# Another order for the first third of an attention and two-MLP kernel

## The chip, the cores and the metric

The kernel runs on one core of a Trainium2 chip. The metric is the device time of one execution in microseconds (us). A core has TensorE (matrix products and transposes, PE in the profile, with its weight loads as PEld), VectorE (DVE), ScalarE (ACT), GpSimd (POOL) and SyncE (SP), which here issues nearly all DMAs. Each engine takes its instructions in the order in which the program gives them and waits where an operand or a buffer isn't ready; the engines run beside each other.

## The reference, cut to what matters

```python
# q, k, v: (2, 8, 768, 64)
k_sum = max of k over blocks of 32;  v_sum = mean of v over blocks of 32
scores_l = q k^T / 8, kept where |i - j| < 16
scores_s = q k_sum^T / 8 + log(32)
a = softmax over [scores_l, scores_s], as exp / (sum + 1e-9)
x = (a @ [v, v_sum]) as (1536, 512)
h = x @ w_in;  x = (h * sigmoid(h)) @ w_out          # d_ff 2048
out = ((x @ w_a) * (x @ w_b)) @ w_out2               # d_ff 1536
```

The weights of the MLPs come in double precision.

## The kernel before, in words

**Attention** runs in 24 steps, 12 for each of the two batches; a step takes 64 queries of all 8 heads against a window of 96 keys and the 24 block maxima. Steps 0 to 7 feed the first block of 512 tokens, 8 to 15 the second, 16 to 23 the third.

**The first MLP** runs in 48 slots, 16 of w_in's columns blocks for each block of tokens: `m1` multiplies x with 128 columns of w_in, `sg` takes the SiLU, `m2` multiplies the gate with 128 rows of w_out. To keep accuracy, each operand is split into a high part (a rounded copy) and a low part (the rest), and a product is three matmuls for each 128 x 128 of weights. Weights come as words of a double: `da` (ScalarE) and `du` (VectorE) decode a tile from its staging buffer, `dj` (VectorE) joins the two, and w_out's tiles are stored to DRAM (`SP`) and loaded again (`RO`) for later blocks of tokens. Decoded tiles share three buffers (`w32`), staged words four (`stage`).

**The order** of all this, up to the last step of the attention and slot 27, is written out by hand as a list of words, `ORDER`, that is run from left to right (lines 28 to 79 and 898 to 923). A word is a name with its numbers, and for many the engine at its end (`a` ScalarE, `v` VectorE, `p` GpSimd). On an engine the instructions stand in the order of the words that put work on it. The names that matter here:

- `LQq`, `LKq`: a quick load of 256 queries or keys of a batch (512 KB, one DMA), reordered by `br`; `LQ`, `LK`: the same in two slower DMAs. `LG`: values for the block means; `LV:n`: the values of step n, into one of four buffers `vw`; `LI`, `LO`: words of a tile of w_in or w_out.
- `tq`, `tk`: transposes of queries and keys on TensorE; `bq` scales queries out of PSUM; `wk` copies keys into windows (ScalarE); `mk`, `sk`, `pk` make block maxima and put them beside the keys.
- `sv`, `mv`, `kv`: block means of v: adds, products, and a copy out of PSUM into the first `vw` buffer; `PV:i` sends it by DMA into buffer i.
- Step n: `sc` scores, `sm` mask and minimum or maximum (VectorE), `su` subtracts it (only for steps outside `ACTS`), `ex` exponentials (ScalarE), `rs` sum plus 1e-9 and reciprocal, `no` multiplies, `tr` transposes, `pc` copies out of PSUM, `av` multiplies with the values, `xh` and `xl` write the high and low part of x.
- `hi`, `lo`: high and low part of a decoded tile; `hR`, `lR`: the same for a tile loaded again; `gh`, `gl`: high and low part of a gate.

For a step in `ACTS`, `ex` is four exponentials, each with its sum and a subtraction folded in; for another it is one, and VectorE sums. In `rs` the 1e-9 stands in a column beside the sums, and one VectorE reduction adds the two:

```python
        nc.vector.tensor_reduce(st[:, 3, :], ap_of(st, NPR, [[1, NPR], [NPR, 2]]), op=ALU.add, axis=AX.X)
        nc.vector.reciprocal(st[:, 3, :], st[:, 3, :])
```

After `ORDER` a loop does slots 28 to 47 and then the second MLP, which forms its products from seven instead of eight block products; its order is not part of the change.

Of the kernel before, what the change touches and what calls it, by code (L numbers as in the profile page):

```python
# [36 lines left out]
av:3 LV:4 no:7:p ex:8 xh:3:v xl:2 tr:4 LV:5 LI:4 LV:7 LV:6 da:in:0 no:6:p pc:5:v sc:9 pc:4:a xl:3 da:in:4 dj:in:1 tr:6  # L37
LI:2 sm:9 sc:11 hi:in:1:a av:5 sm:11 av:4 pc:6:a tr:7 pc:7:a xh:5:a rs:8 LK:1:1 av:6 xh:4:v LO:0 LQ:1:0 lo:in:1:p ex:11
dj:in:0 av:7 hi:in:0:v m1:1:0 xl:5 xh:7:a xl:4 xh:6:v rs:11 du:in:4 xl:6 xl:7 no:8:v LV:8 sc:10 lo:in:0:p sm:10 m1:0:0
m1:1:1 ok:1 tr:8 ex:9 sg:1:p tq:1:0:0 pc:8:a dj:in:4 rs:9 m1:0:1 no:11:v av:8 da:in:2 hi:in:4:a du:in:2 su:10:p du:in:3  # L40
tk:1:1:0 no:9:v LI:6 tr:9 gh:1:p LK:1:2 LO:1 dj:in:2 bq:1:0:0:a tq:1:0:1 da:in:3 LI:8 lo:in:4:v dj:in:3 xh:8:a sg:0:v
# [5 lines left out]
lo:in:5:v gl:2:p m1:6 mk:1:0:0 LI:7 mk:1:2:0 tk:1:0:1 gl:3:v da:out:4 hi:out:3:a lo:out:3:p sg:6:v mk:1:0:1 SP:1 da:in:8
du:out:4 dj:in:8 wk:1:0:1 LO:6 m2:2 m2:3 sk:1:v SP:3 hi:in:8:a pk:1:0:v du:in:7 LO:5 LI:9 dj:out:4 lo:in:8:p wk:1:0:0
da:in:7 LV:11 da:out:6 sc:13 LO:8 dj:in:7 gh:6:v m1:5 du:out:6 gl:6:v du:out:5 dj:out:6 hi:in:7:a lo:in:7:v LI:10
hi:out:4:a m1:8 sm:13 su:13:p sg:5:v sc:14 SP:4 du:in:9 gh:5:a da:in:9 LO:7 gl:5:v LV:9 lo:out:4:v hi:out:6:a lo:out:6:p  # L50
dj:in:9 LV:10 m1:7 du:in:10 sm:14 sc:12 da:out:5 hi:in:9:v lo:in:9:p ex:10 rs:10 no:10:p LG:1:2 sg:8:v m2:4 sg:7:p sm:12
da:in:10 dj:out:5 dj:in:10 av:9 SP:6 hi:out:5:a lo:out:5:v LI:11 LI:13 xh:9:a du:out:8 ex:14 xl:9 da:out:7 gh:8:v m2:5
hi:in:10:v LQ:1:1 du:out:7 gh:7:a sv:1:2:1:p m2:6 rs:14 dj:out:7 SP:5 hi:out:7:a lo:in:10:v lo:out:7:v LG:1:3 da:out:8
ex:12 da:in:13 ex:13 sv:1:3:1:p gl:7:v tr:10 SP:7 dj:out:8 pc:10:a mv:1:2:256:1 du:in:13 LG:1:0 m1:9 sg:9:v gl:8:v
du:in:11 gh:9:a da:in:11 LO:9 sv:1:1:1:p dj:in:13 rs:13 m1:10 du:out:9 dj:in:11 hi:out:8:a av:10 mv:1:3:0:1 lo:out:8:v
LI:12 kv:1:2:a m2:7 xh:10:a LO:13 du:in:12 hi:in:11:a sg:10:v LI:15 hi:in:13:a lo:in:13:p xl:10 da:out:9 SP:8 lo:in:11:v
sc:15 sm:15 tq:1:1:0 pk:1:1:a bq:1:1:0:a dj:out:9 rs:12 hi:out:9:a gh:10:a av:11 du:in:15 gl:9:v m2:8 da:in:12 tq:1:1:1
xh:11:v LO:10 bq:1:1:1:a gl:10:v xl:11 su:15:v no:14:p m1:11 da:in:15 sv:1:0:1:v tr:14 dj:in:15 mv:1:0:256:1 mv:1:1:0:1
LV:12 LO:11 SP:9 kv:1:0:v sg:11:v pc:14:a no:12:p hi:in:15:v m1:13 sc:18 LO:12 gh:11:a pk:1:2:a du:out:10 ex:15 LV:13
dj:in:12 hi:in:12:a lo:out:9:p no:13:v m2:9 sm:18 gl:11:v du:out:11 da:out:10 LI:14 lo:in:12:p sg:13:p tr:12 gh:13:a  # L60
pc:12:a da:out:11 dj:out:11 du:out:13 dj:out:10 PV:1:2 hi:out:10:a lo:in:15:p m1:12 du:in:14 lo:out:10:p PV:1:3 sc:16
LV:14 sm:16 LV:15 da:in:14 rs:15 av:12 SP:10 xh:12:v tr:13 xl:12 hi:out:11:v no:15:v pc:13:a LO:15 LO:14 lo:out:11:v
da:out:13 LV:16 PV:1:1 SP:11 dj:in:14 hi:in:14:v da:out:12 m2:10 lo:in:14:v dj:out:13 av:14 xh:14:a sg:12:v gh:12:v
gl:12:v xl:14 hi:out:13:a tr:15 da:out:14 m1:15 du:out:12 m2:11 gl:13:p pc:15:a dj:out:12 SP:12 sg:15:v hi:out:12:v
av:13 LV:17 lo:out:13:p ex:16 av:15 xh:15:a xl:15 LQ:1:2 SP:13 lo:out:12:p m1:14 du:out:15 da:out:15 du:out:14 gh:15:v
dj:out:14 xh:13:a hi:out:14:v m2:12 sg:14:p xl:13 sc:17 sm:17 gl:15:v m1:17 dj:out:15 gh:14:v sc:19 lo:out:14:p sm:19
# [1069 lines left out]
```

## Time and profile before

| | |
|---|---|
| median of 3 runs | 628.45 us (626.63 to 632.15) |
| profiled execution | 628.75 us, of which span 627.0 us |
| TensorE busy in the span | 608.3 us (97%) |
| VectorE, ScalarE, GpSimd busy | 395.4 us (63%), 294.2 us (47%), 276.1 us (44%) |
| granted TensorE clock, mean | 0.993 of full speed |

The span runs from the first to the last instruction of the profiled execution. The shares are averages over stages with different limits; a busy TensorE may still be waiting inside a group of matmuls. Times below are us from the span's start.

### The profile page before, as it was taken

The numbers are of one execution on the slowest core, as the hardware profiler recorded it, in microseconds if no ns is written. First come the engines' busy times: TensorE is split into PE (matmuls) and PEld (weight loads), VectorE is DVE, ScalarE is ACT, GpSimd is POOL, SyncE is SP. The second block draws the span as 40 slices with busy tenths as digits, with TensorE's granted clock in tenths as the row PEclk, the third lists the DMA queues.
The fourth block names the chain that finished last, engine by engine and source line by source line (L and its number), as shares of the span: only waits on it lengthen the run. The fifth ranks groups of instructions, "written<-read, shape, count | busy, mean of one in ns | idle before, by whom it ended". The sixth has DMA issues, their size and how long they took to land.

```text
span 627.0 us, 10081 instructions
## 1 busy us (share of the span) xinstructions
PE 608.3 (97%) x3630; PEld 525.0 (84%) x3630; DVE 395.4 (63%) x767; ACT 294.2 (47%) x636; POOL 276.1 (44%) x263
## 2 busy tenths in 40 slices
...
GB/s 227 213 238 230 277 271 283 160 179 161 56 38 103 38 98 143 244 204 212 178 160 155 114 51 106 175 158 166 110 227 84 202 35 84 80 217 306 119 0 135
DMA packets 90522, 97.82 MB, mean 156 GB/s; under 512 B 39000, under 2 KB 68440, under 8 KB 90472
## 3 DMA queue, kind: packets, MB, share of 16 engines
...
q14 instruction: 21, 0.17, 0.1%
...
## 4 chain that ended last, share of the span: by engine, by line
PE 88%; DVE 4%; DMA 3%; ACT 3%; issue 1%; SPq 0%; POOL 0%; DVEq 0%; ACTq 0%
PE h L562 20%; PE y L595 19%; PE bankh L806 13%; PE bankg L806 13%; PE ol L853 10%; PE o L832 5%; PE av L466 2%; PE sc L387 1%; PE pt L452 1%; ACT sm L431 1%; DMA vw<-vw 1%; PE kt L259 1%; DMA st_in<-in_moe_w_in_dram 1%; PE qt L259 1%; DMA st_q<-in_q_dram 1%
## 5 line engine op out<-in xcount | busy, mean ns | idle before, releaser
L562 PE MATMUL h<-x,w_in 128*128 128x512 f32 (+1 forms) x600 | 141.7, 386 | 1.1 <-issue 0.9
L595 PE MATMUL y<-g,w_out 128*128 128x512 f32 x576 | 139.8, 394 | 0.8 <-issue 0.8
L595 PEld LDWEIGHTS y<-g,w_out 128*128 128x128 f32 x576 | 106.9, 188 | 25.0 <-issue 2.1
L562 PEld LDWEIGHTS h<-x,w_in 128*128 128x128 f32 x600 | 108.0, 188 | 23.4 <-issue 1.4
L539 POOL TENSOR_TENSOR w_out<-re_out,w_out 128x512 fp32r<-128x512 f32 x36 | 50.5, 1404 | 111.9 <-ACT w_out L148 101.0
L853 PE MATMUL ol<-w_out,plh 128*128 128x512 f32 x192 | 59.1, 389 | 0.0
L577 DVE TENSOR_TENSOR g<-h,g 128x512 fp32r<-128x512 f32 x31 | 21.4, 689 | 39.1 <-ACT g L148 38.9
L539 POOL TENSOR_TENSOR w_out<-w_out,w_out 128x512 fp32r<-128x512 f32 x20 | 27.9, 1407 | 37.0 <-ACT w_out L148 21.8
L570 ACT ACTIVATE h<-h 128x512 f32<-128x512 f32 x31 | 18.1, 584 | 54.7 <-PE h L562 54.7
L853 PEld LDWEIGHTS ol<-w_out,plh 128*128 128x128 f32 x192 | 36.0, 188 | 7.5
L771 POOL TENSOR_TENSOR ab<-sum,ab 128x384 f32<-128x384 f32 x24 | 27.9, 1170 | 30.9 <-DVE sum L768 30.7
L148 ACT CAST w_out<-re_out 128x512 fp32r<-128x512 f32 x37 | 23.0, 622 | 31.4 <-issue 26.0
L853 PE MATMUL ol<-w_out,pll 128*128 128x512 f32 x96 | 37.3, 389 | 0.0
L845 DVE TENSOR_TENSOR pll<-pl,plh 128x1024 fp32r<-128x1024 f32 x12 | 16.9, 1406 | 31.0 <-ACT plh L844 31.0
L832 PE MATMUL o<-w_out,p 128*128 128x512 f32 x108 | 29.9, 394 | 0.0
L516 DVE SCALAR_TENSOR_TENSOR w_out<-w_out,u_out 128x512 uint32<-128x512 uint32 x28 | 24.8, 885 | 7.8 <-ACT w_out L506 6.8
L806 PE MATMUL bankh<-yhT,wab 128*128 128x384 f32 x96 | 28.4, 336 | 0.0
L577 POOL TENSOR_TENSOR g<-sg,g 128x512 fp32r<-128x512 f32 x10 | 13.7, 1378 | 28.4 <-ACT g L148 15.6
L417 DVE CUSTOM_DVE_ANT_0 sm<-sc,mask 128x120 f32<-128x120 f32 x76 | 16.9, 277 | 12.6 <-PE sc L387 12.6
L749 ACT COPY sum<-bankh 128x384 f32<-128x384 f32 x12 | 5.8, 479 | 39.9 <-PE bankh L806 39.9
L683 POOL TENSOR_TENSOR wab<-c,wab 128x768 fp32r<-128x768 f32 x6 | 11.3, 1878 | 28.2 <-ACT wab L680 28.2
L506 ACT ACTIVATE w_out<-st_out 128x512 f32<-128x512 f32 x28 | 18.8, 670 | 6.5 <-DVE w_in L539 3.4
...
## 6 DMA issues: line engine op xcount, KB each, us to landing
...
```

What stands on the lines that cost most here:

```text
L148: nc.scalar.copy(o, i)
L506: nc.scalar.activation(w32, stage_t[kind, f][:, :, 1].bitcast(F32), AF.Prelu, scale=2.0 ** -112, alpha=2.0 ** 32)
L516: nc.vector.scalar_tensor_tensor(bits, bits, 3, u_t.pop((kind, f)), op0=ALU.logical_shift_left, op1=ALU.bitwise_or)
L539: engine.tensor_tensor(w[:, 1], w32_t[kind, f], w[:, 0].bitcast(F32), op=ALU.subtract)
L562: nc.tensor.matmul(h_ps[i][:, cols], win_t[f][:, a, c * P:(c + 1) * P], x_t[n][:, steps, m, c, :], start=(idx == 0), stop=(idx == 3 * NK - 1))
L570: nc.scalar.activation(sg_t[i], ps, AF.Silu)
L577: engines[engine].tensor_tensor(g_t[i][:, 1], sg_t.pop(i), g_t[i][:, 0].bitcast(F32), op=ALU.subtract)
L595: nc.tensor.matmul(y_ps[n, c], wout_t[i][:, a, c * P:(c + 1) * P], g_t[i][:, m, :], start=(f == 0 and (a, m) == (0, 0)), stop=(f == N1 - 1 ...
L771: engines["v" if k == 6 else "p"].tensor_tensor(at, x, at, op=ALU.mult)
L806: nc.tensor.matmul((A, B)[b], weights(u, a, s, s + 1)[:, 0, c * P:(c + 1) * P], yc_t[q, y][m][:, c, :], start=(idx == 0 and not more), sto ...
L832: nc.tensor.matmul(o_ps[t], g[:, a, c:c + P], w[:, m], start=(begins and (a, m) == (0, 0)), stop=(ends and (a, m) == PARTS[-1]))
L853: nc.tensor.matmul(late_o[j], late_p[f][a][:, j * P:(j + 1) * P], wo2_t[N2 + f][:, m], start=(f == 0 and (a, m) == (0, 0)), stop=(f == N2 ...
```

## The change: what it does

The words of `ORDER` are put in another order and some get another engine. Nothing after `ORDER` is changed. In particular:

- The first queries (`LQq:0:0`) are loaded by two DMAs of four heads each instead of one, and `br:q` copies them in two halves (both on ScalarE).
- At the start: `br:k:0:0` comes ahead of `bq:0:0:1` on VectorE, and `bq:0:0:1` moves to ScalarE; `br:k:0:1` moves from ScalarE to VectorE, `bq:0:1:1` from ScalarE to VectorE. On SyncE, `LG:0:0` comes ahead of `LV:0`, and `PV:0:2 PV:0:1 LV:2 LI:3 LV:3 PV:0:3` becomes `PV:0:1 PV:0:2 PV:0:3 LI:3 LV:2 LV:3`.
- Steps 16 and 19 leave `ACTS`: their exponential is one instruction, GpSimd subtracts (`su:16:p`, `su:19:p`), VectorE sums.
- In `rs:6`, `rs:12` and `rs:21` GpSimd adds the 1e-9 between two VectorE instructions.
- The number of words that put work on GpSimd goes from 61 to 77: among them `hi:out:1`, `hi:out:13`, `hR:23`, `hR:26` (high parts of tiles), `gh:17`, `gh:18` (of gates), the low parts `lR:16`, `lR:18`, `lR:20`, `lR:22`, `lR:26`, `lo:in:14`, `gl:26`, the products `no:13` and `no:15`, and the subtractions `su:16`, `su:17`, `su:19`, `su:21`. `hi:out:0` and `gh:1` leave it for ScalarE, `lo:out:2` and `lo:in:8` for VectorE.
- In the middle: `da:out:3`, `gh:2` and `hi:out:3` come ahead of `da:in:5` on ScalarE, and `LI:5` behind `SP:0`, `LK:1:0` and `LO:3` on SyncE. On TensorE the order differs in some places, among them `sc:20 m1:18 av:17` for `sc:20 av:17`, with `m2:14` ahead of `m1:18`.

```diff
-ACTS = {0, 1, 2, 3, 4, 5, 6, 7, 8, 9, 11, 12, 14, 16, 18, 19, 20, 23}
+ACTS = {0, 1, 2, 3, 4, 5, 6, 7, 8, 9, 11, 12, 14, 18, 20, 23}
...
 ORDER = """
-LQq:0:0 br:q:0:0:a LKq:0:0 ok:0 tq:0:0:1 LKq:0:1 LKq:0:2 LG:0:1 bq:0:0:1:v sv:0:1:1:p br:k:0:0:v tk:0:0:1 tk:0:0:0
-tq:0:0:0 br:k:0:1:a mk:0:0:0 tk:0:1:1 mk:0:1:1 wk:0:0:1 LQ:0:1 tk:0:1:0 qz wk:0:0:0 br:k:0:2:v LV:0 tk:0:2:1 mk:0:0:1
+LQq:0:0 br:q:0:0:a tq:0:0:1 ok:0 LKq:0:0 LKq:0:1 LKq:0:2 br:k:0:0:v LG:0:1 bq:0:0:1:a sv:0:1:1:p tk:0:0:1 tk:0:0:0
+wk:0:0:1 br:k:0:1:v tq:0:0:0 tk:0:1:1 mk:0:0:0 tk:0:1:0 mk:0:1:1 LQ:0:1 wk:0:0:0 qz br:k:0:2:v mk:0:0:1 tk:0:2:1
...
-sv:0:2:1:p mv:0:2:0:1 no:2:p kv:0:0:a rs:0 no:0:v pc:1:v PV:0:2 sc:3 tq:0:2:0 tr:0 sc:4 PV:0:1 sm:3 da:in:1 bq:0:2:0:a
-du:in:0 sm:4 ex:3 pc:0:v tq:0:2:1 tr:2 ex:4 sc:7 bq:0:2:1:v av:1 rs:3 no:3:p av:0 tr:3 LV:2 sm:7 rs:5 no:5:p pc:2:a
-xh:1:a rs:4 xh:0:a no:4:p xl:1 sc:6 pc:3:v ex:7 xl:0 sm:6 LI:3 ex:6 rs:7 LV:3 av:2 tr:5 sc:8 sm:8 PV:0:3 xh:2:a rs:6
+sv:0:2:1:p no:2:p pc:1:v mv:0:2:0:1 kv:0:0:a rs:0 sc:3 tq:0:2:0 no:0:v PV:0:1 tr:0 bq:0:2:0:a sc:4 sm:3 ex:3 pc:0:v sm:4
+du:in:0 tq:0:2:1 tr:2 sc:7 ex:4 da:in:1 av:1 rs:3 av:0 PV:0:2 pc:2:a rs:5 no:3:p bq:0:2:1:v tr:3 sm:7 no:5:p rs:4 PV:0:3
+sc:6 LI:3 no:4:p xh:0:a LV:2 LV:3 xh:1:a pc:3:v ex:7 xl:1 sm:6 ex:6 xl:0 rs:7 av:2 xh:2:a tr:5 sc:8 sm:8 rs:6:p av:3
...
-hi:in:6:a SP:0 du:in:5 lo:in:6:v wk:1:2:1 wk:1:2:0 da:out:2 dj:out:2 LK:1:0 LO:3 m2:0 sg:3:p lo:out:1:v hi:out:2:v
-gh:3:a du:in:8 SP:2 lo:out:2:p da:in:5 da:out:3 m2:1 LG:1:1 dj:in:5 hi:in:5:a du:out:3 dj:out:3 tk:1:0:0 gh:2:a
+lo:in:6:v da:out:2 sg:2:p LK:1:0 wk:1:2:0 dj:out:2 m2:0 wk:1:2:1 lo:out:1:v LO:3 hi:out:2:a LI:5 du:in:8 lo:out:2:v SP:2
+da:out:3 du:out:3 LG:1:1 dj:out:3 du:in:5 gh:2:a tk:1:0:0 m2:1 mk:1:0:0 LI:7 gl:2:p m1:6 hi:out:3:a mk:1:2:0 tk:1:0:1
...
-m2:15 yh:0:2 gh:16:p yh:0:0 lR:16:v ex:19 first no:18:p pc:17:v sc:20 sm:20 av:17 rs:19 RO:19 tr:18 gh:18:a LV:21
...
+no:17:v tr:17 gh:16:p first lR:16:p no:16:p pc:17:v no:18:p m2:15 yh:0:2 sc:20 yh:0:0 yh:0:1 sm:20 gl:17:v m1:18 sg:18:p
+yh:0:3 RO:19 av:17 rs:19 tr:18 gh:18:p xh:17:v gl:18:p gl:16:v pc:18:a m1:21 xl:17 no:19:p sc:22 sm:22 RO:23 sg:21:p
...
 """
...
-            nc.sync.dma_start(st, src.rearrange("h (p r) d -> p h (r d)", r=2))
+
+            n = 2 if (kind, b, t) == ("q", 0, 0) else 1
+            for i in range(n):
+                hs = slice(i * H // n, (i + 1) * H // n)
+                nc.sync.dma_start(st[:, hs], src[hs].rearrange("h (p r) d -> p h (r d)", r=2))
...
     def bring(kind, b, t, engine):
-        copy(engine, *quick_t.pop((kind, b, t)))
+        o, i = quick_t.pop((kind, b, t))
+        if kind == "q":
+            copy(engine, o[:, :, 0:H // 2], i[:, :, 0:H // 2])
+            copy(engine, o[:, :, H // 2:], i[:, :, H // 2:])
+        else:
+            copy(engine, o, i)
...
-    def rs(n):
+    def rs(n, engine="v"):
         sm, st, _ = sm_t[n]
         if not by_act(n):
             nc.vector.tensor_reduce(st[:, 1, :], sm, op=ALU.add, axis=AX.X)
-
-        nc.vector.tensor_reduce(st[:, 3, :], ap_of(st, NPR, [[1, NPR], [NPR, 2]]), op=ALU.add, axis=AX.X)
+        if engine == "p":
+            nc.gpsimd.tensor_scalar_add(st[:, 3, :], st[:, 1, :], 1e-9)
+        else:
+
+            nc.vector.tensor_reduce(st[:, 3, :], ap_of(st, NPR, [[1, NPR], [NPR, 2]]), op=ALU.add, axis=AX.X)
         nc.vector.reciprocal(st[:, 3, :], st[:, 3, :])
```

## Rows read from the trace of the kernel before

**Rows 1.** Busy time by stage: us, then engines, granted clock, DMA share, GB/s.

```profile
0.00:45.00 45.00, 35.06 (x458) 28.80 (x459) 33.75 (x125) 33.23 (x127) 22.51 (x46) 0.92 0.98 225
45.00:80.00 35.00, 32.49 (x193) 27.10 (x192) 30.46 (x59) 25.84 (x58) 12.37 (x10) 1.00 0.89 256
80.00:130.00 50.00, 48.68 (x341) 37.88 (x340) 40.25 (x110) 37.35 (x74) 20.50 (x19) 1.00 0.81 233
130.00:180.00 50.00, 48.97 (x358) 38.97 (x359) 28.86 (x92) 29.49 (x64) 18.61 (x15) 1.00 0.37 107
```

**Rows 2.** Waits of TensorE, 42 to 231 us: us, times, longest; three of six.

```profile
PE av L466 <- PE sc L387: 1.4, 2, 0.7
PE kt L259 <- ACT w_out L148: 0.9, 1, 0.9
...
PE y L595 <- issue: 0.8, 1, 0.8
```

**Rows 3.** The chain that ended last: start, us, what.

```profile
0.81 4.12 DMA st_q<-in_q_dram
4.95 1.05 ACT raw_q L148
...
19.40 5.74 ACT sm L431 x32
29.16 6.29 DMA vw<-vw
...
220.66 2.94 PE h L562 x12
...
231.77 2.72 PE h L562 x12
```

**Rows 4.** Timeline of VectorE: start, us, instruction, what it waited for.

```profile
6.74 0.69 DVE L364 TENSOR_SCALAR qb<-qt 128x512 f32<-128x512 f32 x1 [3.58 <-PE qt L259]
7.35 0.78 DVE L150 COPY raw_k<-st_k 128x1024 f32<-128x1024 f32 x1
...
12.16 1.80 DVE L150 COPY raw_k<-st_k 128x1024 f32<-128x1024 f32 x1
...
101.08 1.53 DVE L512 TENSOR_SCALAR u_in<-st_in 128x512 uint32<-128x512 uint32 x1
...
103.13 0.41 DVE L512 TENSOR_SCALAR u_in<-st_in 128x512 uint32<-128x512 uint32 x1
```

**Rows 5.** Timeline of GpSimd.

```profile
12.15 2.93 POOL L321 TENSOR_TENSOR vg<-vg 96x512 f32<-96x512 f32 x3 [3.87 <-DMA vg<-in_v_dram]
...
100.90 6.40 POOL L321 TENSOR_TENSOR vg<-vg 96x512 f32<-96x512 f32 x6 [4.25 <-DMA vg<-in_v_dram]
```

**Rows 6.** Timeline of ScalarE.

```profile
8.58 1.04 ACT L148 COPY raw_k<-st_k 128x1024 f32<-128x1024 f32 x1 [2.59 <-DMA st_k<-in_k_dram]
...
70.51 0.66 ACT L506 ACTIVATE w_out<-st_out 128x512 f32<-128x512 f32 x1 [2.21 <-DMA sp_out<-w_out]
```

**Rows 7.** Busy time in 24 to 28 us, columns as in rows 1.

```profile
24.00:28.00 4.00, 3.73 (x52) 3.02 (x52) 3.71 (x11) 3.93 (x16) 0.98 (x1) 1.00 0.51 86
```

**Rows 8.** Timeline of TensorE.

```profile
25.78 0.66 PE L259 MATMUL qt<-ident,raw_q 128*128 128x128 f32 x4
...
32.53 0.69 PE L466 MATMUL av<-pts,vw 120*64 120x64 f32 x16
...
35.59 0.69 PE L466 MATMUL av<-pts,vw 120*64 120x64 f32 x16 [1.23 <-DMA vw<-vw]
...
168.28 0.69 PE L466 MATMUL av<-pts,vw 120*64 120x64 f32 x16 [0.65 <-PE sc L387]
```

**Rows 9.** Timeline of SyncE's queue.

```profile
25.77 1.66 SPq L344 DMA_DIRECT2D vw<-vw  x2
```

**Rows 10.** GpSimd by form, 0 to 240 us: busy us, mean ns, idle before.

```profile
L150 POOL CAST g<-sg 128x512 fp32r<-128x512 f32 x4 | 3.0, 741 | 20.9 <-PE y L595 17.1 <-ACT sg L570 3.7
...
L181 POOL MEMSET mask<- 128x16 f32 x1 | 0.1, 111 | 0.1
```

More of the change, by code (lines that the diff above doesn't have):

```diff
@@ L37 @@
[L37 to L41, printed above, removed]
@@ L47 @@
[L47 to L51, printed above, removed]
@@ L52 @@
[L52 to L66, printed above, removed]
@@ new lines @@
+du:out:0 gl:0:v da:in:6 tq:1:0:1 hi:in:2:a hi:in:3:a tr:11 tk:1:1:1 mk:1:1:0 pc:11:a gl:1:p du:in:6 LO:2 m1:4 bq:1:0:1:a
+sg:4:p lo:in:3:v da:out:0 dj:in:6 du:out:1 lo:in:2:p da:out:1 gh:4:p boot tk:1:2:1 mk:1:2:1 pc:9:a wk:1:1:0 m1:2
+dj:out:0 hi:out:0:a mk:1:1:1 gl:4:v LO:4 lo:out:0:v tk:1:2:0 dj:out:1 du:out:2 hi:out:1:p m1:3 hi:in:6:a wk:1:1:1 SP:0
+lo:in:6:v da:out:2 sg:2:p LK:1:0 wk:1:2:0 dj:out:2 m2:0 wk:1:2:1 lo:out:1:v LO:3 hi:out:2:a LI:5 du:in:8 lo:out:2:v SP:2
+da:out:3 du:out:3 LG:1:1 dj:out:3 du:in:5 gh:2:a tk:1:0:0 m2:1 mk:1:0:0 LI:7 gl:2:p m1:6 hi:out:3:a mk:1:2:0 tk:1:0:1
@@ new lines @@
+lo:out:3:p da:in:5 sg:3:p gh:3:a gl:3:v dj:in:5 sg:6:v SP:1 hi:in:5:a da:in:8 mk:1:0:1 lo:in:5:v da:out:4 sk:1:v LO:6
+dj:in:8 wk:1:0:1 pk:1:0:v du:out:4 SP:3 du:in:7 LV:11 m2:2 m2:3 LO:5 wk:1:0:0 sc:13 da:in:7 dj:out:4 LO:8 hi:in:8:a
+gh:6:a dj:in:7 lo:in:8:v LI:9 du:out:6 m1:5 du:out:5 gl:6:v hi:in:7:a m1:8 lo:in:7:v hi:out:4:a da:out:6 LI:10 sm:13
+sc:14 su:13:p dj:out:6 du:in:9 sg:5:v gh:5:a gl:5:v da:in:9 SP:4 LO:7 LV:9 hi:out:6:a lo:out:6:p lo:out:4:v dj:in:9
+du:in:10 m1:7 LV:10 sm:14 sc:12 hi:in:9:v da:out:5 ex:10 lo:in:9:p rs:10 no:10:p LG:1:2 m2:4 sg:7:p LI:13 sm:12 da:in:10
@@ new lines @@
+dj:out:5 sg:8:v dj:in:10 hi:out:5:a ex:14 av:9 SP:6 da:out:7 LI:11 lo:out:5:v du:out:8 m2:5 gh:8:v xh:9:v hi:in:10:a
+sv:1:2:1:p du:out:7 dj:out:7 SP:5 lo:in:10:v gh:7:a hi:out:7:a xl:9 lo:out:7:v LG:1:3 sv:1:3:1:p m2:6 da:in:13 ex:12
+da:out:8 ex:13 LQ:1:1 rs:14 gl:7:v tr:10 pc:10:a dj:out:8 SP:7 mv:1:2:256:1 du:in:13 hi:out:8:a LG:1:0 m1:9 sg:9:v
+gl:8:v gh:9:a du:in:11 da:in:11 dj:in:13 LO:9 sv:1:1:1:p rs:13 av:10 dj:in:11 du:out:9 lo:out:8:v m1:10 mv:1:3:0:1
+kv:1:2:a LI:12 LO:13 du:in:12 m2:7 xh:10:a sg:10:v hi:in:11:a hi:in:13:a LI:15 lo:in:13:p xl:10 SP:8 sc:15 gh:10:a
@@ new lines @@
+lo:in:11:v pk:1:1:a sm:15 tq:1:1:0 bq:1:1:0:a da:out:9 dj:out:9 rs:12:p hi:out:9:a du:in:15 gl:9:v da:in:12 sv:1:0:1:p
+m2:8 tq:1:1:1 gl:10:v LO:10 bq:1:1:1:a no:14:p av:11 xh:11:v xl:11 su:15:v m1:11 tr:14 mv:1:0:256:1 LV:12 mv:1:1:0:1
+LO:11 da:in:15 dj:in:15 pc:14:a SP:9 kv:1:0:a sg:11:v LV:13 m1:13 LO:12 no:12:p gh:11:a gl:11:v du:out:10 ex:15
+lo:out:9:p da:out:10 LI:14 sc:18 dj:in:12 hi:in:12:v no:13:p hi:in:15:v LV:14 m2:9 pk:1:2:p sg:13:p du:out:11 sm:18
+gh:13:a lo:in:12:p da:out:11 tr:12 PV:1:3 dj:out:11 du:out:13 pc:12:a dj:out:10 lo:in:15:p hi:out:10:a du:in:14 m1:12
@@ new lines @@
+LO:15 lo:out:10:p sc:16 sm:16 su:16:p PV:1:2 SP:10 rs:15 hi:out:11:a av:12 tr:13 pc:13:a LV:16 xh:12:a lo:out:11:v
+da:out:13 no:15:p xl:12 da:in:14 dj:out:13 PV:1:1 LV:15 dj:in:14 m2:10 hi:in:14:a lo:in:14:p av:14 da:out:12 du:out:12
+sg:12:v xh:14:v gh:12:a xl:14 hi:out:13:p gl:12:v lo:out:13:p tr:15 SP:11 m2:11 pc:15:a LO:14 da:out:14 gl:13:p
+dj:out:12 m1:15 SP:12 av:13 hi:out:12:v LV:17 sg:15:v ex:16 du:out:14 SP:13 av:15 LQ:1:2 xh:15:v lo:out:12:p du:out:15
+xl:15 m1:14 da:out:15 dj:out:14 hi:out:14:v gh:15:v xh:13:a m2:12 xl:13 sg:14:p sc:17 sm:17 gl:15:v m1:17 LV:18 sg:17:p
```

35 lines of the change are left out of this document (18 added, 17 removed).

## The prediction

> **What bounds the kernel now.** I read the table by stage first [rows 1]. The stages shown end at 180 us. From about 220 us on products of 2.72 follow each other without a gap [rows 3], and the whole second half of the program is not touched. Between 45 and 180 us TensorE is busy for some 130 of 135 us. Only up to 45 us does it miss much: 10 us, and part of that at a lower clock (0.92 on average). So the change can give back at most some 15 us, and 6 us of these pass before the first queries are there. VectorE is at 30.46 of 35 us and 40.25 of 50 us in the next two stages, so it comes second; ScalarE lies a little below it.
>
> Then I read who TensorE waited for after 42 us [rows 2]. There are six lines, 5.0 us in all. The three shown are those that the change can reach: a transpose of keys behind ScalarE (0.9), an output product (0.8), and products of weights and values that follow scores (1.4 in two).
>
> Last, the chain that ended last, in its first 36 us [rows 3], of which the first four rows count here. The reader is to see that it hardly runs on TensorE: queries land (0.81 + 4.12), ScalarE reorders them (1.05), VectorE scales their transpose and only then copies keys (0.69 and 0.78 [rows 4]), ScalarE takes exponentials from 19.40 on without a gap, and at the end comes a DMA of value sums. This is the stretch that the new order can shorten.
>
> **The first 19 us.** Today's copy of the first keys on VectorE (0.78 at 7.35 [rows 4]) stands behind `bq:0:0:1`, the 0.69 ahead of it, which waits for the first transposes. The change puts the copy first and moves `bq:0:0:1` to ScalarE, which has nothing else then. Queries, first keys and second keys are equal loads of 512 KB, one behind the other on one queue; the queries had landed at 4.93 [rows 3], the second keys at 8.58 (their copy waited for them [rows 6]), so I put the first keys midway, at 6.75. Gain: 7.35 - 6.75 = 0.6.
>
> The split of the query load adds one DMA issue. ScalarE's 1.05 becomes two halves, the first beside the rest of the load, so queries are ready up to 0.5 earlier. That path is no longer last once the keys' copy doesn't wait for it, so I count it as zero. If the extra issue were to delay the keys, up to 0.6 would be lost and the gain above with it (the range keeps it).
>
> The third keys' copy takes 1.80 instead of 0.78, since it starts at 12.16 while GpSimd adds values from 12.15 on [rows 4, 5]. In the new order VectorE is some 0.6 us earlier there, and the copy is nearly over when GpSimd, which waits for its own load, begins: it ends at about 12.3 instead of 13.96. The second keys' copy moves from ScalarE (1.04) to VectorE (0.78), in time in which VectorE waits for TensorE. A second scaling of queries (0.69 as the first) moves from ScalarE onto VectorE just ahead of the first maxima: it costs that much, but ScalarE loses it where it was the last step before the exponentials. So from 1.66, with 0.3 lost or won by the moved scalings, the exponentials start 1.4 to 1.9 earlier, near 17.6 instead of 19.40.
>
> **From the exponentials to the first product with w_in.** Not all of this is kept. The loads in the queue are the same bytes as before up to `PV`; the queue is well loaded until about 24 us (225 GB/s over the first 45 us [rows 1]) and then drains (86 GB/s from 24 to 28 [rows 7]). The queries of `tq:0:2:0`, transposed at 25.78 [rows 8], are among the last of them, and I put their landing at 24.3. So the gain is capped at 1.5 here.
>
> The value sums end 1.5 earlier too, at 24.2, and with them SyncE's queue comes free: today it sits in front of `PV` until 25.77 [rows 9]. Behind it the order is new: three `PV`, then `LI:3`, then `LV:2` and `LV:3`; before it was two `PV`, `LV:2`, `LI:3`, `LV:3`, `PV`. Each `PV` takes 0.83 to issue (1.66 for two [rows 9]). So `LV:2` goes out 3 x 0.83 + 0.6 = 3.1 (0.6 for `LI:3`, an estimate a little below a `PV`) after the sums, instead of 1.7, and with 512 KB ahead of it. How long it then takes to land is not shown: at most 5.1 before (25.77 + 1.66 = 27.4 [rows 9] to its use at 32.53 without a wait [rows 8]), and 6.29 for the DMA at the end of that queue [rows 3]. So it lands between 24.2 + 3.1 + 5.1 = 32.4 and 33.6. `av:2` would by itself be at 32.53 - 1.5 = 31.0, so it waits 1.4 to 2.6, with transposes, scores and `av:3` queued behind it on TensorE, and `xh:2` and `ex:8` behind it on ScalarE. `av:3` comes 1.83 after `av:2` (35.59 - 1.23 - 32.53), so at 34.2 to 35.4, where it stood at 35.59 after a wait of 1.23 [rows 8]. The gain there is 0.2 to 1.4; I take 1.1, since the later `LV` are no longer mixed in ahead of it and the queue starts empty. From there to 45 us the steps are the same, with swaps of 0.4 to 0.65 on VectorE in either direction, which I count at zero.
>
> **45 to 80 us.** ScalarE waits 2.21 at 70.51 for the store of a decoded tile, with a gate copy and a high part behind it [rows 6], and TensorE's 0.9 [rows 2] ends with that. In the new order the decode of output tile 3 stands ahead of that of input tile 5, so it takes a buffer whose store was issued earlier, and the gate copy isn't behind the wait. Of 0.9 I take 0.6: other sources of the next product end nearly as late. The 0.8 before the first output product is left; its high part goes from GpSimd to ScalarE, between nothing and 0.4 earlier, counted at nothing. The load of input tile 5 and its decode move back past two stores and a load; its product comes only after the fourth output product in both orders, so this costs nothing.
>
> **After 80 us.** At 168.28 `av:17` follows scores after 0.65 of nothing [rows 8]. Now a product with w_in stands between them. One more change between small and large products costs some 0.2 (2.94 behind a small one, 2.72 else [rows 3]), so 0.4 is won. Two steps that leave `ACTS` take one exponential instead of four and give GpSimd one subtraction each. The additions of 1e-9 on GpSimd are not shown for such an operation; the nearest row is a small fill there of 0.111 [rows 10]. The change puts a way to GpSimd and back between two VectorE instructions, with what is queued on VectorE waiting. I take 0.3 each, between nothing and 1.3 when a subtraction of GpSimd is in front. All three stand in stretches where the normalised tile is wanted several us later, so they cost TensorE nothing.
>
> GpSimd gets some 16 pieces more in all: high parts (0.741 for such a cast), low parts, subtractions [rows 10]. What a collision costs is seen at 101.08: VectorE's shift takes 1.53 where others take 0.41, beside the run of GpSimd additions from 100.90 [rows 4, 5]. So some 1.1 of VectorE per collision. Sixteen of these would be 18 us of VectorE, most of them after 130 us, where it idles for 21 of the next 50 us [rows 1]. I count 0.3 for one that lands on the way to a product. [...]
>
> Sum: 1.1 + 0.6 + 0.4 - 0.3 = 1.8 less. Made against the profiled execution (628.75, span 627.0) that is 626.95; the median of the three runs is 0.3 lower, so **626.65**. What is saved early is kept to the end only if VectorE, at nearly nine tenths up to 130 us, follows; hence I do not add the larger ends together.
>
> **The rivals.**
> *All of it is kept.* `LV:2` lands in time, so 1.5 at `av:3`, 0.9 at 74 us, 0.8 at the first output product and 0.6 at the scores: 3.8 less, 624.65. For it: the queue starts empty. Against it: VectorE's load up to 130 us.
> *The transfers and the decoding decide.* The front gain ends in a wait further on, at 64 to 74 or at 103 us, where TensorE already waits on stores and on VectorE: 628.4, no change. For it: 30.46 of 35.
> [...] Three collisions of 1.1 on the way to output products between 80 and 160 us, where products follow without a gap: -1.8 + 3.3, so 630.0. Against it: the idle VectorE time.
> *Slower by `LV:2`.* If the sums don't end earlier than today (25.7, because ScalarE's exponentials are not sooner), `LV:2` lands at 25.7 + 3.1 + 6.29 = 35.1, `av:3` comes at 36.95 instead of 35.59, 1.4 later, and with nothing else won it is 629.9. It decides from the point at which the end of the sums plus the landing time passes 30.6 (35.59 - 1.83 - 3.1).
>
> **How the numbers follow.** Forecast (625.3 to 627.8) 0.45; all kept (623 to 625.3) 0.17; no change (627.8 to 629) 0.17; GpSimd 0.08; `LV:2` 0.10; something not seen here 0.03. The range 623.2 to 630.2 takes the forecast, no change, most of all kept and most of the two slower ones. Measurement can tell about 1%, 6.3 us; none of the cases reaches it, so the chances are 0.05 faster (ends of the second case and below), 0.90 within 1%, 0.05 slower.
>
> **What would show it.** The first keys' copy on VectorE near 6.7, the third's near 0.8 long; exponentials from 17.6; `PV` issued near 24.2; a wait of `av:2` for `vw`, none of `av:3`; no 2.21 on ScalarE near 70; no gap ahead of `av:17`; first output product of tile block 2 (the dense stretch from 220 us) 1 to 3 us earlier. The prediction is wrong if the keys land late behind the split queries, if `av:2` waits over 3 us, or if TensorE has new waits for GpSimd after 130 us.

## The result, and the profile after

The change made the kernel slower: 633.48 us (median, 630.11 to 636.27) against 628.22 for the kernel before (626.35 to 632.15), a ratio of 1.0076 [1.0063, 1.009]. The forecast was 626.65 with a range to 630.2, so the time lies above the range, and the sign is the other one. The profiled execution has a span of 634.1 us against 627.0; it is 2.4 above the median of its kernel, so its 7.1 more are a little above the 5.3 between the medians.

The page of the changed kernel, the costliest group of instructions (busy us, mean ns, then idle time ahead of them and what ended it), and below it who TensorE waited for from 42 to 240 us (us, times, longest):

```profile
span 634.1 us, 10072 instructions
...
L574 PE MATMUL h<-x,w_in 128*128 128x512 f32 (+1 forms) x600 | 144.0, 390 | 4.0 <-DVE g L589 4.0
```

```profile
PE h L574 <- DVE g L589: 4.0, 1, 4.0
PE av L478 <- DMA vw<-in_v_dram: 1.2, 1, 1.2
PE qt L268 <- PE sc L396: 0.8, 1, 0.8
PE av L478 <- PE sc L396: 0.6, 1, 0.6
PE y L607 <- ACT w_out L148: 0.2, 1, 0.2
```

Three waits of before are gone or smaller [rows 2]: the 0.9 for a high part and one of the two behind scores, as forecast, and the 0.8 before the first output product, which the prediction counted at nothing. In their place stands one of 4.0, for VectorE, which the kernel before has nowhere, and one of 1.2 for values, at 45.21, just ahead of the first product with w_in. The timeline shows where (start, duration, engine, line, what; up to 20 us the front, then the stretch from 112 to 127 us, then two places that the prediction named):

```profile
1.83 3.21 SPq L248 DMA_DIRECT2D st_k<-in_k_dram  x3
...
7.36 0.77 DVE L150 COPY raw_k<-st_k 128x1024 f32<-128x1024 f32 x1 [4.21 <-DMA st_k<-in_k_dram]
...
11.90 0.69 DVE L150 COPY raw_k<-st_k 128x1024 f32<-128x1024 f32 x1 [0.60 <-DMA st_k<-in_k_dram]
...
19.48 0.40 ACT L440 ACTIVATE sm<-sm,st 128x120 f32<-128x120 f32 x1 [0.40 <-DVE st L426]
...
70.72 0.68 ACT L518 ACTIVATE w_out<-st_out 128x512 f32<-128x512 f32 x1 [1.26 <-DMA st_out<-in_moe_w_out_dram]
...
112.93 2.97 POOL L330 TENSOR_TENSOR vg<-vg 96x512 f32<-96x512 f32 x3
...
115.62 4.90 DVE L524 TENSOR_SCALAR u_in<-st_in 128x512 uint32<-128x512 uint32 x1
...
115.87 1.93 POOL L458 TENSOR_TENSOR sm<-sm,st 128x480 f32<-128x480 f32 x2
...
117.76 1.26 POOL L551 TENSOR_TENSOR w_out<-w_out,w_out 128x512 fp32r<-128x512 f32 x1
118.98 0.98 POOL L458 TENSOR_TENSOR sm<-sm,st 128x480 f32<-128x480 f32 x1
119.91 0.34 POOL L150 COPY kin<-ks 128x192 f32<-128x192 f32 x1
120.19 0.54 POOL L150 COPY kout<-ks 128x192 f32<-128x192 f32 x1
120.45 1.27 DVE L589 TENSOR_TENSOR g<-h,g 128x512 fp32r<-128x512 f32 x2
121.18 5.19 PE L574 MATMUL h<-x,w_in 128*128 128x512 f32 x12 [4.01 <-DVE g L589]
...
175.48 0.69 PE L478 MATMUL av<-pts,vw 120*64 120x64 f32 x16
```

Read it from the bottom of the knot. The product `m1:11` starts at 121.18 after 4.01 of nothing, because the bank of PSUM that it fills is in use until VectorE has done the gate's low part `gl:9`, the first of the pair at 120.45 (the eighth experiment shows this). `gl:9` and `gl:10` stand on VectorE behind the shift `du:in:15`, which takes 4.90 instead of 0.41 [rows 4]. And beside this shift GpSimd goes from one instruction into the next with hardly a gap: sums of values, two products (`no`, the normalised softmax tiles), a low part, a product, two copies of keys, from 112.93 to 120.73. Three of these steps are new on GpSimd there: `sv:1:0:1` (VectorE before), `no:13` (VectorE) and `pk:1:2` (ScalarE).

Busy time by stage, and in steps of 2 us around the knot (columns as in rows 1; the third number from the end is the granted clock):

```profile
0.00:45.00 45.00, 34.66 (x398) 28.19 (x398) 30.23 (x117) 29.97 (x113) 20.98 (x44) 0.85 0.93 206
...
80.00:130.00 50.00, 45.08 (x289) 34.72 (x291) 37.95 (x88) 33.68 (x68) 23.18 (x24) 0.93 0.78 224
...
116.00:118.00 2.00, 1.17 (x21) 0.86 (x19) 2.00 (x1) 1.88 (x4) 2.00 (x3) 1.00 1.11 331
118.00:120.00 2.00, 0.00 (x0) 0.00 (x0) 2.00 (x1) 0.00 (x0) 2.00 (x3) 0.77 0.88 222
120.00:122.00 2.00, 0.82 (x2) 0.73 (x3) 2.00 (x4) 0.00 (x0) 0.73 (x2) 0.50 1.03 313
122.00:124.00 2.00, 2.00 (x6) 1.52 (x6) 1.64 (x4) 0.00 (x0) 0.00 (x0) 0.50 0.51 193
124.00:126.00 2.00, 2.00 (x7) 1.58 (x6) 0.00 (x0) 0.00 (x0) 0.00 (x0) 0.53 0.02 6
```

While TensorE waits its granted clock falls to 0.50 (0.77 over the window from 118 to 120) and stays there until about 126 (0.53 over the last window), and `m1:11` takes 5.19 where the same product takes 3.02 in the first experiment below, with the clock at 1.00. The wait and the slow product are 4.0 + 2.2 = 6.2 of the 7.1 by which the span is longer. At 115.95 us, just ahead of it, the changed kernel was only 0.6 behind (the same transpose stands at 115.39 in the kernel before; `av:11` was done by then there and was still to come here, so without its wait `m1:11` would have started 1.4 later than before, at 117.17 against 115.74).

The front gained nothing in this execution either: the first keys' copy at 7.36 (before 7.35), exponentials from 19.48 (before 19.29 in the same view; the chain has them from 19.40 [rows 3]).

### The profile page after: what moved, and what is told of

The parts are those of the page before. It is cut to its first block, busy times and chain, and to the rows that moved or that the text cites. A ratio compares the mean times of both kernels' runs of the same rounds, so it can differ in the third digit from the quotient of the medians.

```text
span 634.1 us, 10072 instructions
## 1 busy us (share of the span) xinstructions
PE 614.0 (97%) x3630; PEld 529.3 (83%) x3630; DVE 388.5 (61%) x752; ACT 291.5 (46%) x621; POOL 290.5 (46%) x282
## 4 chain that ended last, share of the span: by engine, by line
PE 85%; DMA 5%; DVE 4%; issue 2%; ACT 2%; SPq 1%; POOL 0%; ACTq 0%; DVEq 0%
PE h L574 18%; PE y L607 18%; PE bankh L818 13%; PE bankg L818 13%; PE ol L865 10%; PE o L844 5%; DMA sp_out<-w_out 2%; DMA vw<-in_v_dram 2%; PE av L478 2%; PE sc L396 2%; PE pt L464 1%; DMA raw_q<-in_q_dram 1%; DVE u_in L524 1%; PE vsum L344 1%; SPq L248 1%
## 5 line engine op out<-in xcount | busy, mean ns | idle before, releaser
L574 PE MATMUL h<-x,w_in 128*128 128x512 f32 (+1 forms) x600 | 144.0, 390 | 4.0 <-DVE g L589 4.0
L574 PEld LDWEIGHTS h<-x,w_in 128*128 128x128 f32 x600 | 109.6, 191 | 27.0 <-DVE g L589 4.3
L551 POOL TENSOR_TENSOR w_out<-re_out,w_out 128x512 fp32r<-128x512 f32 x39 | 54.7, 1404 | 116.1 <-ACT w_out L148 103.1
L551 POOL TENSOR_TENSOR w_out<-w_out,w_out 128x512 fp32r<-128x512 f32 x19 | 26.4, 1398 | 20.4 <-ACT w_out L148 15.9
L330 POOL TENSOR_TENSOR vg<-vg 96x512 f32<-96x512 f32 (+2 forms) x19 | 17.9, 942 | 11.5 <-DMA vg<-in_v_dram 10.4
L582 ACT ACTIVATE sg<-h 128x512 f32<-128x512 f32 x18 | 10.7, 597 | 26.5 <-PE h L574 24.2
```

Of the source, the lines that this page charges most:

```text
L330: engines[engine].tensor_tensor(t[0:KL, :, 0:m, :], t[0:KL, :, 0:m, :], t[0:KL, :, m:2 * m, :], op=ALU.add)
L551: engine.tensor_tensor(w[:, 1], w32_t[kind, f], w[:, 0].bitcast(F32), op=ALU.subtract)
L574: nc.tensor.matmul(h_ps[i][:, cols], win_t[f][:, a, c * P:(c + 1) * P], x_t[n][:, steps, m, c, :], start=(idx == 0), stop=(idx == 3 * NK - 1))
L582: nc.scalar.activation(sg_t[i], ps, AF.Silu)
```

## Experiments

Ratios are to the kernel before, timed beside each. "The changed kernel" is the one with the whole change. Words of the order are written as in the code: `sv:1:0:1:p` is a step and the engine that does it (v VectorE, p GpSimd, a ScalarE).

**1. Undo three engines.** Edit of the changed kernel:

```
-sv:1:0:1:p  no:13:p  pk:1:2:p
+sv:1:0:1:v  no:13:v  pk:1:2:a
```

> The changed kernel with three words given back their engines of before: the value sums sv:1:0:1 and the product no:13 from GpSimd to VectorE, the maxima copy pk:1:2 from GpSimd to ScalarE. Theory A (a nearly unbroken run of GpSimd work from 111 to 120.7 us holds one VectorE shift for 4.90 us, and TensorE waits 4.0 us behind it and then runs 5 us at the lower clock): the shift takes under 1.6 us, TensorE's wait near 117 us is under 0.5, and the time falls by 4 to 7 us, to 627 to 630. Rival B (the new order of the first 45 us, in which TensorE ran at the lower clock from 13 to 26 us, is what lasts): the wait near 117 us goes, but products come no earlier at 130 us, and the time stays above 632.

Measured: 628.51, ratio 1.0002 [0.9977, 1.0028]. The timeline of this kernel:

```profile
113.92 0.43 DVE L524 TENSOR_SCALAR u_in<-st_in 128x512 uint32<-128x512 uint32 x1
...
114.26 0.68 DVE L589 TENSOR_TENSOR g<-h,g 128x512 fp32r<-128x512 f32 x1
...
115.69 3.02 PE L574 MATMUL h<-x,w_in 128*128 128x512 f32 x12
```

The shift takes 0.43, the product starts without a wait. Three words of some hundreds carry the loss.

**2 and 3. Front of one kernel, rest of the other.** The two orders do the same steps in their first 185 words, so they can be cut there.

```
second: ORDER = before[:185] + after[185:], queries in one part
third:  ORDER = after[:185] + before[185:], ACTS as before
```

> The first 185 words as before (up to the first products with w_in, about 45 us, with the first queries in one load), all others as changed. Theory A: the front was only some 3 us late and was caught up by 115 us, so the loss stays: 631 to 635, with the long VectorE shift near 115 us still there. Rival B: the front is the loss: 627 to 629.

> The first 185 words as changed (with the first queries in two loads), all others and the set of steps with four exponentials as before. Theory A: 627.5 to 630, at most 1.5 over before, although the first products with w_in come 2 to 3 us later. Rival B: 632 to 635, as the whole change.

Measured: 634.44, ratio 1.009 [1.0058, 1.0122], and 628.95, ratio 1.0015 [0.9995, 1.0036]. In the first the shift takes 4.91 and TensorE waits 4.11. So the loss doesn't come from the front; but the new front doesn't gain the 1.1 that it had in the sum either.

**4. The three steps moved in the kernel before.**

```
-sv:1:0:1:v  no:13:v  pk:1:2:a
+sv:1:0:1:p  no:13:p  pk:1:2:p
```

> The kernel before with only the three words of the first experiment moved to GpSimd (sv:1:0:1, no:13, pk:1:2); nothing else is changed. Theory A: GpSimd's work near 115 us joins into one run of 6 us or more, a VectorE shift or copy is held for 3 us or more, and the time rises by 2 to 6 us. Rival C (the three moves are not enough alone, the order of the words around them is needed too): within 1 us of before, and no VectorE instruction over 2 us.

Measured: 628.61, ratio 0.9997 [0.9976, 1.0019]: no loss. In the timeline of this kernel (the sums shown one by one):

```profile
111.82 1.75 POOL L321 TENSOR_TENSOR vg<-vg 96x512 f32<-96x512 f32 x1
...
112.62 1.24 DVE L512 TENSOR_SCALAR u_in<-st_in 128x512 uint32<-128x512 uint32 x1
...
113.65 0.81 POOL L321 TENSOR_TENSOR vg<-vg 96x256 f32<-96x256 f32 x1
...
116.91 1.29 POOL L539 TENSOR_TENSOR w_out<-w_out,w_out 128x512 fp32r<-128x512 f32 x1
116.97 2.73 DVE L516 SCALAR_TENSOR_TENSOR w_in<-w_in,u_in 128x512 uint32<-128x512 uint32 x1 [0.23 <-ACT w_in L506]
118.16 0.98 POOL L446 TENSOR_TENSOR sm<-sm,st 128x480 f32<-128x480 f32 x1
```

GpSimd's run is as long, but the shift came early. It was issued during the first sum, which ends at 113.57; the second sum, which needs its result, starts 0.08 later, at 113.65; and the shift ends at 113.86, that is 0.29 after the end of the first. A later join (116.97) is held across two instructions: the product at 118.16 follows the low part without a gap (it starts 0.04 before the low part's recorded end), and the join takes 2.73, to 0.56 after the product's end at 119.14. The gates were done by then, so TensorE didn't wait. So moving the steps isn't enough; it counts which instruction is held, for how long, and what stands behind it. In the changed kernel the shift was issued at 115.62, in the last of the three sums (115.12 to 115.90), and the products followed that without a gap.

**5 to 8. What is held, for how long, and who waits.** Four edits of the changed kernel, each alone:

```
fifth:   du:in:15 moved behind xl:11, so gl:9 and gl:10 go first
sixth:   sv:1:0:1:p -> sv:1:0:1:v
seventh: no:13:p -> no:13:v, pk:1:2:p -> pk:1:2:a
eighth:  sg:9:v -> sg:9:p  (SiLU into a tile of SBUF, bank free at once)
```

> The changed kernel with one word moved: the shift of word block 15 (du:in:15) stands behind the residual of state 11 (xl:11) instead of ahead of the gates' low parts gl:9 and gl:10. All three steps stay on GpSimd, so its run of instructions is as long as in the changed kernel. If the loss is a VectorE shift that waits out that run with the low parts queued behind it, TensorE's 4.0 us wait for the low part before m1:11 goes, the stretch from 118 to 126 us keeps the high clock, and the time is 628 to 629 us. If the loss is GpSimd's longer run itself, whatever stands on VectorE, another VectorE instruction is held in the shift's place and the time stays at 633 to 634.

> The changed kernel with only the sums of values (sv:1:0:1) back on VectorE; the product no:13 and the two key copies pk:1:2 stay on GpSimd. If the hold lasts as long as GpSimd's run goes on after the shift is issued, this removes the 3 us with which the run began and lets the shift go first, at about 114 us, as in the kernel with all three back: no wait of TensorE over 0.5 us there and 628 to 629 us. If each step moved adds its own share, about 630 to 631 us remain.

> The changed kernel with no:13 back on VectorE and pk:1:2 back on ScalarE, but the sums sv:1:0:1 still on GpSimd. If the hold is as long as the rest of GpSimd's run, it is shorter by what those two took at its end (0.98 and 0.7 to 0.8 us): the shift takes 3.0 to 3.4 us instead of 4.90, TensorE's wait before m1:11 falls from 4.0 to 2.2 to 2.6 us, and the time is 630 to 632 us. If the hold ends with one GpSimd instruction, whichever is under way, the shift is held 1 to 2 us and the time is 628 to 629.

> The changed kernel with one letter changed: the ninth SiLU (sg:9) writes to a tile of SBUF instead of in place to its PSUM bank, so that the bank which m1:11 fills is free when ScalarE has read it, and not only when VectorE has done the low part gl:9. GpSimd's run and the order on VectorE are those of the changed kernel. If the loss reaches TensorE by this bank alone, the shift is still held 4 to 5 us but TensorE does m1:11 without the wait of 4.0 us; the second product of block 9 then waits for the low part where m1:11's work doesn't cover it, so the time is 628 to 631 us. If the held VectorE queue reaches TensorE in several ways, the wait moves to another product and the time stays above 632.

| edit | median us | ratio | shift took | wait ahead of m1:11 |
|---|---|---|---|---|
| none | 633.48 | 1.0076 [1.0063, 1.009] | 4.90 | 4.01 |
| shift later | 628.99 | 1.0003 [0.9976, 1.0029] | 2.31 | none |
| sums back | 627.64 | 0.9989 [0.9971, 1.0008] | 0.43 | none |
| the other two back | 631.79 | 1.0052 [1.0022, 1.0082] | 3.68 | 2.54 |
| bank free | 629.05 | 1.0016 [0.9985, 1.0047] | 4.93 | none |

Timeline of the kernel with the shift later, then of the one with the other two back, then of the one with the bank free:

```profile
112.54 1.25 DVE L589 TENSOR_TENSOR g<-h,g 128x512 fp32r<-128x512 f32 x2
...
114.28 3.02 PE L574 MATMUL h<-x,w_in 128*128 128x512 f32 x12
...
115.20 2.31 DVE L524 TENSOR_SCALAR u_in<-st_in 128x512 uint32<-128x512 uint32 x1
```

```profile
111.70 3.68 DVE L524 TENSOR_SCALAR u_in<-st_in 128x512 uint32<-128x512 uint32 x1
...
113.83 1.26 POOL L551 TENSOR_TENSOR w_out<-w_out,w_out 128x512 fp32r<-128x512 f32 x1
...
116.03 4.61 PE L574 MATMUL h<-x,w_in 128*128 128x512 f32 x12 [2.54 <-DVE g L589]
```

```profile
116.86 4.93 DVE L524 TENSOR_SCALAR u_in<-st_in 128x512 uint32<-128x512 uint32 x1
...
118.31 3.02 PE L574 MATMUL h<-x,w_in 128*128 128x512 f32 x12
...
121.72 0.82 DVE L589 TENSOR_TENSOR g<-sg,g 128x512 fp32r<-128x512 f32 x1
...
124.04 0.67 PE L344 MATMUL vsum<-vg,sel 96*120 96x128 f32 x4 [2.27 <-issue]
```

Each link of the chain is cut by itself here. Order: with the low parts first, GpSimd's run is the same and the loss is gone. Length: with two steps fewer at the end of the run, the hold ends 0.3 after that run does (113.83 + 1.26 = 115.09; the shift ends at 115.38), and the wait shrinks with it, from 4.01 to 2.54; the rival by which the hold ends with the one instruction under way falls for this place. The seventh shift measured 3.68, above the 3.0 to 3.4 expected. Reach: with the bank free the shift is held as long as ever, and `m1:11` doesn't wait. TensorE isn't free of the hold, though: it waits 2.27 at 124.04, ahead of the block means. The profile names no releaser; VectorE ended `xl:11`, which was queued behind the held shift, 0.11 before (123.93). This second way costs less: the clock stays at 1.00 there, and the product behind it takes 2.99.

A hold doesn't always last to the end of a run, however. Later in the trace of the changed kernel two low parts stand back to back on GpSimd, and a shift beside them (below, the second low part by itself in the last line):

```profile
131.31 2.77 POOL L551 TENSOR_TENSOR w_in<-w_in,w_in 128x512 fp32r<-128x512 f32 x2 [10.58 <-DVE w_in L150]
131.41 1.51 DVE L524 TENSOR_SCALAR u_out<-st_out 128x512 uint32<-128x512 uint32 x1
...
132.61 1.47 POOL L551 TENSOR_TENSOR w_in<-w_in,w_in 128x512 fp32r<-128x512 f32 x1
```

The shift ends at 132.92, while the second low part still runs: it was held over one instruction only, although the next one followed without a gap. The trace has 18 such places (shifts of 0.49 to 1.55, each ending 0.28 to 0.29 after the first instruction), with low parts and sums, most of them in the second MLP. At the knot the shift ended only 0.3 after the first of the two key copies or after the end of the run. In six kernels where a shift was held there (the changed one and experiments 2, 5, 7, 8 and 14), it was passed over at 25 ends of a GpSimd instruction that the next one followed without a gap, and at each of them one of the two was a `no` product. So the length of the run is not enough to tell the hold. That the products make the difference is only read from the traces: no run tests it, it isn't shown why they would, and they may not be alone in it (a shift of 0.72 at 46.27 was passed over between a low part and two small fills).

**9 to 11. Where the forecast gain stayed.** With the loss repaired the kernels stand at 1.000, not at 0.997. So both repairs were put together, and then one part of the change at a time taken back:

```
ninth:    du:in:15 behind xl:11, sv:1:0:1:v
tenth:    the ninth, first queries loaded and copied in one part
eleventh: the ninth, rs:6:p rs:12:p rs:21:p -> rs:6 rs:12 rs:21
```

> Both repairs at once: the changed kernel with the shift du:in:15 behind xl:11 and the sums sv:1:0:1 on VectorE. If the reordering of the rest gains what the prediction summed (1.8 us), it stands free here: 626 to 627 us, ratio 0.996 to 0.998. If the front and the rest give nothing on the path, the time is that of the kernel before, ratio 0.999 to 1.001.

> The kernel with both repairs, but the first queries loaded and copied in one part, as before the change. If the two parts are worth nothing (the prediction counted zero), the ratio to the kernel before agrees with that of the two-part kernel beside it within 0.15%. If the second load ahead of the keys delays them, this one is faster by up to 0.6 us (0.1%) and the first copy of keys starts near 6.7 instead of 7.3 us.

> The kernel with both repairs, but the 1e-9 of steps 6, 12 and 21 added on VectorE again (the reduction of 0.16 us in place of GpSimd's addition of 0.22). If these additions cost nothing (the prediction said that TensorE doesn't see them), the ratio agrees with that of the kernel with both repairs within 0.15%. If they delay the reciprocal behind GpSimd's queue where TensorE needs it, this one is faster by 0.5 to 1 us.

Measured: 627.53, ratio 0.999 [0.9978, 1.0002]; 625.99, ratio 0.9965 [0.9944, 0.9987]; 627.44, ratio 0.9991 [0.9975, 1.0006]. No cost of the 1e-9 on GpSimd is seen. The load in one part is faster than the kernel before. Timeline of the front of the ninth, then of the tenth:

```profile
1.83 3.20 SPq L248 DMA_DIRECT2D st_k<-in_k_dram  x3
...
7.08 0.82 DVE L150 COPY raw_k<-st_k 128x1024 f32<-128x1024 f32 x1 [3.94 <-DMA st_k<-in_k_dram]
...
17.93 0.40 ACT L440 ACTIVATE sm<-sm,st 128x120 f32<-128x120 f32 x1
```

```profile
1.30 3.54 SPq L248 DMA_DIRECT2D st_k<-in_k_dram  x3
...
6.79 0.78 DVE L150 COPY raw_k<-st_k 128x1024 f32<-128x1024 f32 x1 [3.65 <-DMA st_k<-in_k_dram]
...
17.11 0.41 ACT L440 ACTIVATE sm<-sm,st 128x120 f32<-128x120 f32 x1
```

The second half of the queries is one more issue on SyncE's queue, and the keys go out 0.53 later. In one part, the first copy starts at 6.79 and the exponentials at 17.11.

**12 to 14. The queries in one or two parts elsewhere.**

```
twelfth:    the fifth (shift later), queries in one part
thirteenth: the kernel before, queries in two parts
fourteenth: the changed kernel, queries in one part
```

> The kernel whose shift du:in:15 stands behind xl:11 (sums still on GpSimd; ratio 1.0003 when measured), now with the first queries loaded and copied in one part. If the second part's load costs by delaying the issue of the keys from 1.30 to 1.83 us, this one gains what the kernel with both repairs gained by it: ratio 0.996 to 0.998, exponentials from about 17 us in place of 18 to 18.5. If that gain was chance, the ratio is again 0.999 to 1.001.

> The kernel before with nothing changed but the first queries loaded and copied in two parts. If the split delays the keys on the path, the keys are issued 0.5 us later and the time is 0.5 to 1.5 us more: ratio 1.001 to 1.0025. If its cost was chance, or the front of the kernel before hides it behind the copies of its keys (which share ScalarE with the queries), ratio 0.999 to 1.001.

> The changed kernel with the first queries loaded and copied in one part, and the held shift left in. If the costs add up, the 1.5 to 3 us that one part gained in the two repaired kernels come off here too: 630.5 to 632 us, ratio 1.004 to 1.006, and TensorE still waits some 4 us before m1:11. If an earlier front only makes TensorE wait longer at the held shift, the ratio stays at 1.0075.

Measured: 625.96, ratio 0.9958 [0.9942, 0.9975]; 628.1, ratio 0.9996 [0.9976, 1.0016]; 632.23, ratio 1.0077 [1.0053, 1.0102]. The gain comes again on the other repaired kernel. The kernel before doesn't feel the split. And in the changed kernel, with the held shift left in (4.90, wait 4.06), one part doesn't gain: the two causes are not shown to add. Its profiled execution, with exponentials from 17.41, was the shortest of its six (630.37; the others lie between 631.65 and 634.27), so whether an earlier front is lost again at the held shift isn't settled.

**15 and 16. Which half of the split.** The fifth kernel with one of the two alone:

```
fifteenth: n = 1 (one load), two copies
sixteenth: n = 2 (two loads), one copy
```

> The kernel whose shift stands behind xl:11, with the first queries loaded by one DMA but copied in two halves. If the second DMA's issue, which puts the keys' issue from 1.30 to 1.83 us, is what costs, this kernel is as fast as the one with one load and one copy: ratio 0.996 to 0.998. If the two copies cost, it is at 0.999 to 1.001.

> The same kernel with the first queries loaded by two DMAs but copied in one piece. If the second DMA's issue costs, the keys are issued at 1.83 us, their first copy starts at 7.1 to 7.9 us, and the ratio is 0.999 to 1.001. If the copies are what costs, it is at 0.996 to 0.998.

Measured: 626.43, ratio 0.9974 [0.9961, 0.9986], and 626.98, ratio 0.9983 [0.9965, 1.0002]. One load with two copies stays ahead of the kernel before, so the two copies alone don't take the gain. Two loads with one copy can't be told from no change, but its interval also holds the other's ratio. Over all repaired kernels: with one load 0.9965, 0.9958 and 0.9974; with two 1.0002, 1.0003, 0.9989, 0.999, 0.9991 and 0.9983 (the first, fifth, sixth, ninth, eleventh and sixteenth). Every one of the first group lies below every one of the second, and the means differ by 0.0027, some 1.7 us; three pairs give 1.6 (tenth and ninth), 2.8 (twelfth and fifth, which were not timed together) and 0.6 (fifteenth and sixteenth). In all profiles of the new front with one load the first keys' copy starts at 6.79 to 6.96 and the exponentials at 17.11 to 17.75 (four kernels); with two loads at 7.08 to 8.29 and at 17.93 to 19.68 (ten kernels, the changed one among them).

## Why the prediction was wrong, step by step

**The step that failed** is the pricing of GpSimd's pieces: "So some 1.1 of VectorE per collision", "I count 0.3 for one that lands on the way to a product". The row from which it came [rows 4, 5] is one hold, and its length was taken for that of any collision. At 101.08 the first sum had run from 100.90 for 1.42, to 102.32, and the shift ended at 102.61, again 0.29 after the end of that one instruction. Most holds of these traces are like that: of the 29 shifts that took over 0.6 in the changed kernel, 27 ended 0.28 to 0.29 after the one GpSimd instruction under way (1.51 at 131.41 is one). The one that decided was not: beside a run with `no` products it lasted over five more instructions, 4.90 - 0.41 = 4.5, four times as long. The seventh experiment shows it shrinking with the run; why the shift ends after one instruction at one place and not at another stays open.

Two figures of the prediction are loose, but nothing hangs on them: VectorE "at nearly nine tenths up to 130 us" is busy for 0.87 of the time from 45 to 80 us and 0.81 from there on [rows 1], and 19.40 less 1.66 is 17.7, not 17.6.

**The rival with this mechanism** (three collisions of 1.1 between 80 and 160 us, 630.0) had the stretch and the sign, and a chance of 0.08; it named output products, and the wait fell on a product with w_in. What spoke "against it: the idle VectorE time" was the second error: idle time elsewhere doesn't help when the gate's low parts are already queued behind the held shift, and the bank that TensorE needs next hangs on them (fifth and eighth experiments). One collision did it. Nothing in the sum had the clock of 0.50 after the wait: 2.2 more for one product (1.4 in the fourteenth experiment, where it took 4.39).

**The query split, counted at zero**, was the third. The prediction named the alternative: "If the extra issue were to delay the keys, up to 0.6 would be lost and the gain above with it". That is what the profiles show: keys issued 0.53 later, first copy at 7.36 instead of 6.75. In the kernels with one load it is at 6.79 to 6.96, so the midway estimate was good, and the exponentials at 17.11 to 17.75 meet the forecast of 17.6. In the changed kernel they started at 19.48. How 0.53 of issue grows into some 1.7 us at the end isn't shown.

**Right.** The third keys' copy takes 0.69 (forecast about 0.8; 1.80 before [rows 4]). ScalarE's wait of 2.21 at 70.51 [rows 6] is gone from there (1.26 at 70.72, for another load), and TensorE's 0.9 with it; in the second experiment, with the same order there behind the old front, TensorE waits 0.83 for a high part at 67.60 again, so it isn't shown that this part of the order is what removed it. `av:17` follows its predecessor at 175.48 without the 0.65 [rows 8]. The 1e-9 additions took 0.22 (forecast 0.3), and no cost of them is seen (eleventh experiment). The repaired kernels with one load end where the forecast lay: 625.96, 625.99 and 626.43 against 626.65. So the reordering as a whole was worth about what the sum said, though its terms are not shown one by one; the split took the gain and the held shift went far beyond it.

**Half right.** `av:2` waited 1.05 for its values (forecast 1.4 to 2.6), `av:3` waited 0.84 where none was forecast, and another product with values 1.25 at 45.21. `PV` was issued at 28.52 in place of 24.2 in this execution, in which TensorE's clock stood at 0.50 from about 13 to 26 us; in the tenth kernel it was 23.97. Such a stretch came in some profiled executions of either kind of front (the mean clock from 13 to 30 us is 0.60 in this one and 0.84 in the twelfth kernel) and not in others (1.00 in the fifth and the tenth), and most of it was made up between 45 and 116 us (3.2 behind at the first product with w_in, 0.6 at 115.95); what sets it off isn't settled.
